# Attention with a threshold, then a feed-forward block: one eviction for both banks of a pair's turned queries or keys

## The chip, the cores and the metric

The kernel runs on one core of one Trainium2 chip. A core has a matrix engine (TensorE, PE in the profile; its weight loads stand apart as PEld), a vector engine (VectorE, DVE), a scalar engine (ScalarE, ACT), GpSimd (POOL) and a queue that issues most transfers (SyncE, SP). Each engine works through its own instructions in order, and waits on semaphores for the others. Matmul results land in PSUM, which has eight banks of 512 fp32 columns on 128 partitions; other engines evict them from there into on-chip memory (SBUF). The metric is the device time of one execution in microseconds (us).

## The reference

Everything is fp32. The attention keeps only scores within `tau` of their row's maximum:

```python
# q, k, v: batch 8, heads 8, sequence 576, head size 64
scores = scale * np.matmul(q, k.transpose(0, 1, 3, 2))       # scale = 1/8
thresh = np.max(scores, axis=-1, keepdims=True) - tau
scores = np.where(scores >= thresh, scores, -1000000000.0)
attn = np.exp(scores - np.max(scores, axis=-1, keepdims=True))
attn = attn / (np.sum(attn, axis=-1, keepdims=True) + 1e-09)
out = np.matmul(attn, v)
# the heads are joined to x: 4608 rows x 512
h = np.maximum(x @ w_in, 0.0)                                # w_in 512 x 2048
result = h * h @ w_out                                       # w_out 2048 x 512
```

## The kernel before

The first half of the time is the attention, the second the feed-forward block, which the change doesn't touch. All of this is about the attention.

Two heads of one batch make a *pair* (32 pairs). A *unit* is 128 query rows of a pair; a pair has four whole units, and the 64 queries that are left over from two neighbouring pairs share a fifth, so two pairs make nine units, 144 in all. In the code `FULL` is 4, `MAIN` 512, `REST` 64 and `HALF` 64. Units go two by two, an even one (A) and an odd one (B), through a pipeline of 72 *periods* and a few at its ends. What one period does for a unit is cut into named steps, and a step table says in which order the steps are written in the program; every engine meets its own part of them in that order. A `-` behind a step means that it belongs to the period before, `--` to the one before that. There are two tables. `CONVERTING` serves the first half of the attention (periods 2 to 34), in which weights are converted from wide floats on the side; `PLAIN` serves the rest. This is `PLAIN`, with steps among them that no later section speaks of:

```python
PLAIN = """
    put give fetch ahead eU-- powA0-- V-- powA1-- eV-- maskA1-- PV-- powB1-- c1- RA- powB0-- T--
    maskA0-- U- W-- Q-- x-- c4- maskB1-- SA- eT-- RB- maskB0-- topA0- over- topA1- c2 s2 leastA- eW--
    SB- topB0- s1- c5 c6 topB1- inv- leastB- xm-- c3
""".split()
```

The steps, with the lines that the profile shows them under:

- **T, the turn** (L423, TensorE). Scores need queries and keys with the head's 64 numbers on the partitions, so a pair's queries (8 transposes) or keys (10, with the left-over queries among them) are transposed into the middle columns of PSUM banks 1 and 4. One turn is done in most periods; 64 in all.
- **eT** (L428, L436, ACT) evicts the turn. Queries: two scaled copies of 256 columns (L428), one from each bank, which multiply by 1/8 and the sign. Keys: a copy of 256 columns from bank 1, one of 320 from bank 4 (L436), and a scaled copy of the 64 left-over queries from bank 1 (L428).
- **SA, SB** (L459, TensorE): a unit's scores against the first 512 keys. A's two heads land in banks 0 and 5, B's in banks 2 and 3. **RA, RB** (L459): against the last 64 keys, into the edges of banks 1 and 4, beside the main columns.
- **topA0 to topB1** (L477, DVE): copy a head's scores out of PSUM and give the row minimum of the negated scores. **pow** (L487, ACT) and **mask** (L492, DVE): exponential and threshold.
- **U, V** (L403, TensorE) transpose most of the weights into the two banks of a tile `pt`; **eU, eV** (L552, ACT) evict them. **W** (L403) transposes the rest into banks 2 and 3, **Q** (L542) spreads the row sums beside them, and **eW** (L552, from `sc`) evicts both.
- **PV** (L561, TensorE): weights times values, in banks 0 and 5. **x** (L708 ACT, L710 DVE) evicts the result, **xm** (POOL) scales it.

The tile `sc` is banks 0 to 5. Its order is kept by the function `touch`. Every instruction on `sc` reports there which banks it uses, as a range `on`. `touch` walks back through the last 300 reports of the other engines. An instruction whose banks don't overlap is declared independent; of those that overlap, the latest of each engine becomes a dependence, reads against reads too. The test for overlap is:

```python
if on[-1] < others[0] or others[-1] < on[0]:
```

It compares the first and the last bank of the two ranges.

## Time and profile before

| what | value |
|---|---|
| median of 3 runs | 1271.97 us (1270.42 to 1272.17) |
| span of the profiled execution, first to last instruction | 1273.4 us |
| attention, by the last values matmul | ends near 494 us |
| converting table | about 25 to 248 us |
| plain table | about 250 to 490 us |
| granted TensorE clock, mean | 0.996 |

The profiled execution's own time outside the span is not given on the page; its span is 1.4 us over the median of the plain runs. The profile has several views. The page gives each engine's busy time. The chain of waits follows the work that ended last back from the end, at each step to what released it. The timeline lists instructions in order of time, with neighbours of one kind merged; a bracket behind a row names how long the engine was idle before it and what ended that. Groups by shape gives count, busy time and mean length of one kind of instruction. Busy by stretch sums each engine over a window. A transpose or a score matmul in fp32 shows as two instructions, so counts on TensorE are twice those of the program. On ACT and DVE one row's start commonly lies about 0.1 us before the end of the row ahead, since the engine takes up the next while the last one's results still land.

### The profile page before, as it was taken

To read this page: it belongs to the slowest core of one execution; us is meant where nothing else is said; L and a number is where in the kernel's file an instruction comes from. 1 tells how busy PE (TensorE), PEld (TensorE's weight loads), DVE (VectorE), ACT (ScalarE), POOL (GpSimd) and SP (SyncE) were. 2 spreads that over 40 slices of the span, in tenths; PEclk is the share of its full clock that TensorE was granted. 3 is DMA by queue.
4 is the path that set the end of the run, shared out by engine and by line. 5 is a ranking of instruction groups with operands and counts; after the bars stand their busy time and mean duration, and the time that the engine had idled before them with its cause. 6 is when DMAs were issued, how large, how long until landed. Compare 5 with 4: busy or idle time off the path is not lost.

```text
span 1273.4 us, 55161 instructions
## 1 busy us (share of the span) xinstructions
PE 1251.7 (98%) x22991; PEld 1093.6 (86%) x22991; DVE 988.2 (78%) x2385; ACT 844.3 (66%) x1536; POOL 982.5 (77%) x1070
## 2 busy tenths in 40 slices
PE   8999999999999999999999999999999999999998
PEld 5777776777777778988888888999999999999998
DVE  6999998999999996886887878867746654665463
ACT  6999998999999994666765856675524432443240
POOL 2999998877776542988898989868787878787776
PEclk8999999999999999999999999999999999999999
DMA  7566677434333323657667657579965336533511
GB/s 186 143 161 154 167 198 188 120 89 107 89 81 89 83 53 97 192 166 237 202 191 231 215 169 249 172 274 369 267 163 152 83 107 163 146 84 107 167 35 35
DMA packets 289912, 196.79 MB, mean 155 GB/s; under 512 B 98560, under 2 KB 250624, under 8 KB 289664
## 3 DMA queue, kind: packets, MB, share of 16 engines
q1 hardware_dynamic: 288352, 192.86, 52.8%
q8 instruction: 181, 2.97, 1.0%
q14 instruction: 67, 0.55, 0.1%
q10 hardware_dynamic: 1312, 0.41, 0.1%
HBM read 120.85 MB, written 72.35 MB: 152 GB/s over the span
## 4 chain that ended last, share of the span: by engine, by line
PE 72%; DMA 3%; ACT 2%; POOL 2%; DVE 1%; issue 1%; DVEq 0%; ACTq 0%; POOLq 0%; SPq 0%
PE po L818 27%; PE ph L997 17%; PE ph L818 10%; PE sc L561 7%; PE sc L459 6%; PE pt L403 4%; PE sc L542 1%; PE sc L423 1%; POOL arena L126 1%; DMA g<-arena 1%; ACT arena L970 1%; DVE arena L126 1%; DMA w<-arena 1%; ACT arena L971 1%; ACT c L857 1%
## 5 line engine op out<-in xcount | busy, mean ns | idle before, releaser
L126 POOL TENSOR_TENSOR arena<-arena 128x512 f32<-128x512 f32 (+1 forms) x314 | 378.7, 1224 | 125.1 <-DVE arena L126 113.5
L818 PE MATMUL po<-wall,arena 128*64 128x128 f32 x7056 | 385.8, 273 | 1.4 <-ACT arena L813 0.8
L818 PEld LDWEIGHTS po<-wall,arena 128*64 128x64 f32 x7056 | 385.1, 137 | 1.9 <-ACT arena L813 1.0
L126 DVE TENSOR_TENSOR arena<-ph,arena 128x512 f32<-128x512 f32 x378 | 254.5, 688 | 77.4 <-PE ph L997 30.9
L123 POOL TENSOR_TENSOR arena<-arena 128x128 f32<-128x128 f32 (+1 forms) x322 | 265.5, 826 | 24.1 <-DMA arena<-w 8.5
L997 PE MATMUL ph<-arena,wall 128*128 128x256 f32 x1176 | 256.7, 380 | 2.3 <-DVE arena L126 2.1
L997 PEld LDWEIGHTS ph<-arena,wall 128*128 128x128 f32 x1176 | 222.4, 190 | 36.3 <-DVE arena L126 6.2
L126 DVE TENSOR_TENSOR arena<-po,arena 128x128 f32<-128x128 f32 x378 | 107.6, 288 | 159.3 <-PE po L818 151.4
L492 DVE SCALAR_TENSOR_TENSOR arena<-arena 128x576 f32<-128x576 f32 x288 | 225.9, 820 | 0.4 <-ACT arena L487 0.3
L487 ACT ACTIVATE arena<-arena 128x576 f32<-128x576 f32 x288 | 214.1, 781 | 13.4 <-DVE arena L477 13.3
L477 DVE TENSOR_SCALAR_CACHE_REDUCE arena<-sc 128x576 f32<-128x576 f32 x288 | 203.4, 752 | 18.5 <-ACT arena L552 5.7
L857 ACT COPY c<-arena 128x512 f32<-128x512 f32 (+1 forms) x295 | 168.9, 578 | 70.1 <-DVE arena L123 36.1
L459 PE MATMUL sc<-arena 64*64 64x512 f32 (+1 forms) x2304 | 179.6, 415 | 5.6 <-ACT arena L552 1.2
L561 PE MATMUL sc<-arena 64*64 64x128 f32 (+1 forms) x5760 | 165.6, 261 | 1.0 <-ACT arena L552 0.5
L123 DVE TENSOR_TENSOR arena<-arena,c 128x512 f32<-128x512 f32 x235 | 154.2, 664 | 12.1 <-ACT c L857 7.1
L561 PEld LDWEIGHTS sc<-arena 64*64 64x64 f32 x5760 | 150.4, 133 | 4.5 <-ACT arena L552 0.7
L552 ACT COPY arena<-pt 128x1024 f32<-128x1024 f32 x143 | 145.0, 1014 | 4.6 <-PE pt L403 3.9
L459 PEld LDWEIGHTS sc<-arena 64*64 64x64 f32 x2304 | 76.8, 134 | 71.4 <-issue 47.2
L813 ACT COPY arena<-po 128x128 f32<-128x128 f32 x63 | 16.6, 264 | 177.6 <-PE po L818 174.8
L818 PE MATMUL ph<-arena,wall 128*64 128x128 f32 x2352 | 129.2, 273 | 0.6 <-DVE arena L710 0.6
L818 PEld LDWEIGHTS ph<-arena,wall 128*64 128x64 f32 x2352 | 128.3, 137 | 1.4 <-issue 1.0
L484 POOL TENSOR_SCALAR arena<-arena,tau_p 128x2 f32<-128x2 f32 x144 | 83.8, 582 | 58.5 <-DVE arena L477 44.7
(55 smaller groups left out, 1142.5 us busy)
## 6 DMA issues: line engine op xcount, KB each, us to landing
gp<-arena SPq DMA_DIRECT2D x96, 256.0 KB, 3.4
arena<-gp SPq DMA_DIRECT2D x96, 256.0 KB, 5.4
w<-arena SPq DMA_DIRECT2D x60, 256.0 KB, 2.7
wall<-w SPq DMA_DIRECT2D x49, 256.0 KB, 5.3
g<-arena SPq DMA_DIRECT2D x48, 256.0 KB, 3.7
arena<-g SPq DMA_DIRECT2D x48, 256.0 KB, 5.0
arena<-w SPq DMA_DIRECT2D x44, 256.0 KB, 3.4
arena<-in_v_dram SPq DMA_DIRECT2D x32, 288.0 KB, 3.8
```

The costliest lines, as they stand in the source:

```text
L123: e.tensor_tensor(out=out, in0=x, in1=y, op=ALU.subtract)
L126: e.tensor_tensor(out=out, in0=x, in1=y, op=ALU.add)
L459: made = nc.tensor.matmul(sc[at, ds(to, count)], lhs, kT[rows, ds(at_k, count)], start=True, stop=True)
L477: made = nc.vector.tensor_scalar(out=s[:, j, :], in0=sc[:, ds(at, S)], scalar1=1.0, scalar2=None, op0=ALU.mult, op1=ALU.min, accum_out=nmx ...
L484: nc.gpsimd.tensor_scalar(out=thr, in0=nmx, scalar1=tau_p[:, :], scalar2=None, op0=ALU.add)
L487: nc.scalar.activation(out=w[:, :, j, :], in_=of(j), func=AF.Exp, bias=nmx[:, j : j + 1], scale=-1.0)
L492: nc.vector.scalar_tensor_tensor(out=w[:, :, j, :], in0=of(j), scalar=thr[:, j : j + 1], in1=w[:, :, j, :], op0=ALU.is_le, op1=ALU.mult, a ...
L552: touch(kind, copy_by(joined(to), whole(pt, 0, count)), at, 2 * BANK, m)
L561: made = nc.tensor.matmul(sc[ds(u * D, D), ds(5 * j * BANK + row, count)], loaded_v[i][rows, (c - (u != j)) % CH, :], wT[m][rows, ds(weigh ...
L818: nc.tensor.matmul(to[cols], lhs[:, cols], rhs, start=start, stop=stop, skip_group_check=True)
L857: nc.scalar.copy(c, y)
L997: nc.tensor.matmul(to[:, 2 * j : 2 * j + 2, :], W_IN[m, k][:, ts(2 * h + j, P)], part_x(steps, k, m), start=(not more and j == 0), stop=Tr ...
```

## The change

The two banks' pieces of a turn are evicted by one instruction. For this, keys and left-over queries share one tile: `kT` now has two parts of 320 columns, the first with 256 keys and the 64 left-over queries, the second with 256 keys and the last 64. The left-over queries are therefore copied unscaled, and the units that use them take their scale in the row minimum, from the tile `qscale` in place of the constant 1.0. Score matmuls read the first 512 keys as two pieces of 256 that lie 320 apart. The new eviction tells `touch` its banks with the pair `(1, 4)`. Only the very first keys' turn is still evicted in two pieces, one of them on DVE.

```diff
-                sb.tile([P, S], FP32, tag="kT", bufs=K_RING, name="kT"),
-                sb.tile([P, REST], FP32, tag="qR", bufs=K_RING, name="qR"),
+                sb.tile([P, MAIN + 2 * REST], FP32, tag="kT", bufs=K_RING, name="kT"),
...
-    def touch(what, made, at, size, key=0):
+    def touch(what, made, at, size, key=0, on=None):
...
-        on = range(at // BANK, (at + size - 1) // BANK + 1)
+        on = on or range(at // BANK, (at + size - 1) // BANK + 1)
...
-    def turn(i, which, spots, other=None):
+    def turn(i, which, spots, joint=None, other=None):
...
-        def scaled(to, spot):
-            touch(kind, nc.scalar.activation(out=to, in_=spot[0], func=AF.Identity, scale=qscale[:, :]), spot[1], BANK, i)
+        n = half + which * REST
+        into = to[which].rearrange("p (r n) -> p r n", r=2)
+        by_scale = lambda out, in_: nc.scalar.activation(out=out, in_=in_, func=AF.Identity, scale=qscale[:, :])
+        copies = [nc.scalar.copy if which else by_scale, other]
 
         def then():
-            part = lambda r, x, n: (spots[r][0][:, ds(x, n)], spots[r][1])
-            if which:
-                for r, n in ((0, half), (1, half + REST)):
-                    spot = part(r, 0, n)
-                    copy_by = other if r and other else nc.scalar.copy
-                    touch(kind, copy_by(to[1][:, ds(r * half, n)], spot[0]), spot[1], BANK, i)
-                scaled(to[2], part(0, half, REST))
-                ask_ahead(i, 1)
+            if joint is None:
+                for r, (spot, at) in enumerate(spots):
+                    touch(kind, copies[r](into[:, r, :], spot[:, 0:n]), at, BANK, i)
             else:
-                for r in range(2):
-                    scaled(to[0][:, ds(r * half, half)], part(r, 0, half))
-                ask_ahead(i, 0)
+                touch(kind, copies[0](into, joint[:, :, 0:n]), spots[0][1], BANK, i, (1, 4))
+            ask_ahead(i, which)
...
-                qT, kT, qR = turned[of[c]]
-                lhs = qT[rows, ds((c * FULL + t) * HALF, HALF)] if t < FULL else qR[rows, :]
+                qT, kT = turned[of[c]]
+                lhs = qT[rows, ds((c * FULL + t) * HALF, HALF)] if t < FULL else kT[rows, ds(MAIN // 2, REST)]
+                keys, into = kT[rows, ds(MAIN + REST, REST)], sc[at, ds(to, count)]
+                if not rest:
+                    keys = kT[rows, :].rearrange("p (r n) -> p r n", r=2)[:, :, 0 : MAIN // 2]
+                    into = into.rearrange("p (r n) -> p r n", r=2)
...
+        unscaled = qscale[:, :] if units[n][1] == FULL else 1.0
...
-                out=s[:, j, :], in0=sc[:, ds(at, S)], scalar1=1.0, scalar2=None,
+                out=s[:, j, :], in0=sc[:, ds(at, S)], scalar1=unscaled, scalar2=None,
...
-            free = None
+            free, both_ = None, sc.rearrange("p (r n) -> p r n", r=2)[:, :, ds(BANK + REST, (FULL + 1) * HALF)]
...
-            late["turn"] = [turn(g // 2, g % 2, free or spots()) for g in turns]
+            late["turn"] = [turn(g // 2, g % 2, free or spots(), both_) for g in turns]
```

No step changes its place in a table. What changes on the engines is which instruction waits for which. In the changed kernel line numbers are lower by one or two: L706 is the copy x, L550 the evictions eU, eV and eW, L485 the exponential, L458 the scores, L540 Q, L402 the weights' transposes; L436 and L428 are the new single evictions of keys and queries.

ACT before, in the plain table, from x of a period with a keys' turn to the exponentials of the next unit (the names in brackets are the engines whose semaphores an instruction waits for):

```order
L708 COPY arena<-sc 128x128 [waits DMAHW5_49,DMAHW4_49,PE_49]
L436 COPY arena<-sc 128x256 [waits PE_49]
L436 COPY arena<-sc 128x320 [waits PE_49]
L428 ACTIVATE arena<-sc,qscale 128x64
L552 COPY arena<-sc 128x2x4x64 [waits PE_49,Pool_49]
L552 COPY arena<-pt 128x2x8x64 [waits Activation_49]
L487 ACTIVATE arena<-arena 128x9x64 [waits DVE_49] x2
```

ACT now, at the same place:

```order
L706 COPY arena<-sc 128x128 [waits DMAHW5_49,DMAHW4_49,PE_49]
L436 COPY arena<-sc 128x640 [waits PE_49]
L550 COPY arena<-sc 128x2x4x64 [waits Pool_49]
L550 COPY arena<-pt 128x2x8x64 [waits Activation_49]
L485 ACTIVATE arena<-arena 128x9x64 [waits DVE_49] x2
```

Three evictions have become one. The two old ones waited for the last transposes of the turn into their bank; the wait of the new one is for the last matmul of Q, and eW behind it (L550 from `sc`) no longer waits for TensorE. Of the program's 72 such eW, 31 have lost that wait.

TensorE before, at the same place, from W to the first transposes of V:

```order
L403 MATMUL sc<-ident,arena 128x64 x4
L542 MATMUL sc<-ident,arena 64x64 [waits DVE_49]
L542 MATMUL sc<-ident,arena 64x64 x7
L459 MATMUL sc<-arena 64x512 [waits Activation_49]
L459 MATMUL sc<-arena 64x512
L459 MATMUL sc<-arena 64x512 [waits DVE_49]
L459 MATMUL sc<-arena 64x512
L459 MATMUL sc<-arena 64x64 [waits Activation_49]
L459 MATMUL sc<-arena 64x64
L459 MATMUL sc<-arena 64x64 [waits Activation_49]
L459 MATMUL sc<-arena 64x64
L459 MATMUL sc<-arena 64x512 [waits Activation_49]
```

TensorE now:

```order
L402 MATMUL sc<-ident,arena 128x64 x4
L540 MATMUL sc<-ident,arena 64x64 [waits DVE_49]
L540 MATMUL sc<-ident,arena 64x64 x7
L458 MATMUL sc<-arena 64x512 [waits Activation_49]
L458 MATMUL sc<-arena 64x512
L458 MATMUL sc<-arena 64x512 [waits DVE_49]
L458 MATMUL sc<-arena 64x512
L458 MATMUL sc<-arena 64x64 [waits Activation_49]
L458 MATMUL sc<-arena 64x64 x3
L458 MATMUL sc<-arena 64x512 [waits Activation_49]
```

Nothing moved: SA (two heads), RB, SB. RB waited for the evictions of banks 1 and 4 one by one and now waits once, for the one eviction; SB waits for eW, as before.

ACT before, in the converting table, at a queries' turn:

```order
L487 ACTIVATE arena<-arena 128x9x64 [waits DVE_49]
L487 ACTIVATE arena<-arena 128x9x64
L428 ACTIVATE arena<-sc,qscale 128x256 [waits DVE_49] x2
L708 COPY arena<-sc 128x128 [waits DMAHW4_49,DMAHW3_49,PE_49]
L708 COPY arena<-sc 128x128 [waits PE_49]
```

ACT now, at the same place:

```order
L485 ACTIVATE arena<-arena 128x9x64 [waits DVE_49]
L485 ACTIVATE arena<-arena 128x9x64
L428 ACTIVATE arena<-sc,qscale 128x512 [waits DVE_49]
L706 COPY arena<-sc 128x128 [waits DMAHW4_49,DMAHW3_49,PE_49]
L706 COPY arena<-sc 128x128 [waits PE_49]
```

Here each of the two old evictions waited for the row minimum that read its own bank, the third and the fourth of a period; the new one waits for the fourth.

More of the change, by code (lines that the diff above doesn't have):

```diff
@@ L450, in scores @@
         of, t = units[n]
-        at_k, count = (MAIN, REST) if rest else (0, MAIN)
+        count = REST if rest else MAIN
         for j in range(2):
@@ L456, in scores @@
                 rows, at = ds(j * D, D), ds(c * HALF, HALF)
-                qT, kT, qR = turned[of[c]]
-                lhs = qT[rows, ds((c * FULL + t) * HALF, HALF)] if t < FULL else qR[rows, :]
-                made = nc.tensor.matmul(
-                    sc[at, ds(to, count)], lhs, kT[rows, ds(at_k, count)], start=True, stop=True
-                )
+                qT, kT = turned[of[c]]
[4 more added lines that the diff above has]
+                    into = into.rearrange("p (r n) -> p r n", r=2)
+                made = nc.tensor.matmul(into, lhs, keys, start=True, stop=True)
                 touch("scores" if t < FULL else "last scores", made, to, count, of[c])
@@ L690, in turn_some @@
         def turn_some():
[L691 removed]
+            free, both_ = None, sc.rearrange("p (r n) -> p r n", r=2)[:, :, ds(BANK + REST, (FULL + 1) * HALF)]
             if turns and p < 2:
                 pq = pt_pool.tile([P, 2, BANK], FP32, tag="pt", name="pq")
[L694 to L695 removed]
+                free, both_ = [(pq[:, r, :], None) for r in range(2)], pq
+            late["turn"] = [turn(g // 2, g % 2, free or spots(), both_) for g in turns]
         def PV():
@@ L1203 @@
             pq = pt_pool.tile([P, 2, BANK], FP32, tag="pt", name="pq")
-            turn(0, 0, [(pq[:, r, :], None) for r in range(2)])()
+            turn(0, 0, [(pq[:, r, :], None) for r in range(2)], pq)()
             keep_busy(8, sc[:, ds(5 * BANK, P)])
-            turn(0, 1, spots(), nc.vector.tensor_copy)()
+            turn(0, 1, spots(), None, nc.vector.tensor_copy)()
             for p in range(FIRST_PERIOD, NU // 2 + 6):
```

1 line of the change is left out of this document (removed).

## The prediction

> **What bounds the kernel now.** I first read the busy shares by stretch, to part the attention half into its two step tables, then the chain of waits, then the timeline of single periods, and last the groups by shape for the durations. The two rows are the stretch of the converting table and of the plain table (columns: stretch and its length, then PE, PEld, DVE, ACT and POOL busy, granted clock, DMA share, GB/s).
>
> ```profile
> 60.00:180.00 120.00, 116.50 (x3031) 87.52 (x3024) 118.62 (x333) 117.65 (x217) 110.66 (x123) 1.00 0.65 165
> 255.00:466.00 211.00, 210.59 (x5691) 158.21 (x5695) 202.43 (x595) 198.85 (x340) 141.44 (x189) 1.00 0.38 87
> ```
>
> In the converting stretch DVE (118.62 of 120) and ACT (117.65) are both nearly full. In the plain stretch TensorE has 210.59 of 211, ACT 198.85. A busy TensorE alone proves little, since its ends are modelled, so I look at the chain over part of two plain periods (start, length, what):
>
> ```profile
> 321.00 0.46 PE sc L423 x10
> 321.45 0.50 PE pt L403 x16
> 321.95 0.12 PE sc L403 x4
> 322.08 0.39 PE sc L542 x16
> 322.47 1.85 PE sc L459 x24
> 324.32 0.64 PE pt L403 x16
> 324.96 2.24 PE sc L561 x68
> ```
>
> Each piece starts where the one before ends: turn (L423), U (L403), W (L403 into sc), Q (L542), scores SA, RB and SB (L459), V, values. No other engine is in the chain, so in the plain stretch anything that stops TensorE is added to the time, and anything that only relieves ACT is worth nothing there. ACT around the same keys' turn, then the TensorE rows that go with it, then DVE's first row minimum (timelines: start, length, engine, line, shapes):
>
> ```profile
> 321.59 0.25 ACT L708 COPY arena<-sc 128x128 f32<-128x128 f32 x1
> 321.74 0.71 ACT L436 COPY arena<-sc 128x256 f32<-128x256 f32 x2
> 322.32 0.34 ACT L428 ACTIVATE arena<-sc,qscale 128x64 f32<-128x64 f32 x1
> 322.59 0.58 ACT L552 COPY arena<-sc 128x512 f32<-128x512 f32 x1
> 323.07 1.02 ACT L552 COPY arena<-pt 128x1024 f32<-128x1024 f32 x1
> 324.35 0.78 ACT L487 ACTIVATE arena<-arena 128x576 f32<-128x576 f32 x1 [0.27 <-DVE arena L477]
> ...
> 322.01 0.46 PE L542 MATMUL sc<-ident,arena 64*64 64x64 f32 x16
> 323.26 0.63 PE L459 MATMUL sc<-arena 64*64 64x512 f32 x4
> 324.25 0.28 PE L403 MATMUL pt<-ident,arena 64*128 64x64 f32 x2
> ...
> 323.55 0.76 DVE L477 TENSOR_SCALAR_CACHE_REDUCE arena<-sc 128x576 f32<-128x576 f32 x1 [0.24 <-issue]
> ```
>
> The reader is to see that today the turn's three evictions fill exactly the time in which TensorE does U, W and Q: they begin at 321.74, long before Q ends at 322.47, and are over at 322.66. Then eW (L552 from sc) starts at 322.59, 0.12 after Q's end; SB starts at 323.26, after eW's end at 323.17; and V at 324.25, after eU's end at 324.09. DVE waits 0.24 and ACT 0.27 a period; they have that much to spare.
>
> **The change, part by part.** *The new wait, plain stretch.* The order rows in the section on the change show the cause. The one eviction is noted as lying on banks 1 to 4, which takes in banks 2 and 3, where W and Q write just ahead of it in program order. Its wait for TensorE is therefore for Q's last matmul and not for the turn's; eW, which carries that wait today (where nothing stands ahead of it, it idles for Q, 2.6 us in all in the groups below), has lost it. Behind the waiting eviction on ACT stand eW and eU, and SB waits for eW, V for eU. The durations, from the groups of ACT over 255 to 466 us and one group of the whole run:
>
> ```profile
> L552 ACT COPY arena<-pt 128x1024 f32<-128x1024 f32 x66 | 66.3, 1005 | 0.0
> L552 ACT COPY arena<-sc 128x512 f32<-128x512 f32 x33 | 19.3, 585 | 3.0 <-PE sc L542 2.6
> L428 ACT ACTIVATE arena<-sc,qscale 128x256 f32<-128x256 f32 x30 | 12.7, 477 | 0.0
> L436 ACT COPY arena<-sc 128x320 f32<-128x320 f32 x15 | 6.6, 440 | 0.0
> ...
> L813 ACT COPY arena<-ph 128x512 f32<-128x512 f32 x63 | 36.7, 582 | 81.4 <-PE ph L997 37.3 <-PE ph L818 35.1 <-DVE arena L126 8.9
> ```
>
> Copies of 512 and 1024 columns take 0.585 and 1.005 us, so a column costs 0.82 ns. The keys' eviction of 640 columns is then 0.585 + 128 x 0.82 ns = 0.69 us, the scaled queries' of 512 is 0.477 + 256 x 0.82 ns = 0.69 us as well. A copy of 512 columns out of two banks (L552, 585 ns) costs what one out of a single bank does (L813, 582), so I add nothing for the second bank. What a restart of TensorE costs is shown where ACT is late today, at the first plain turn (ACT, then two rows of TensorE):
>
> ```profile
> 252.60 0.61 ACT L552 COPY arena<-sc 128x512 f32<-128x512 f32 x1
> ...
> 253.26 0.66 PE L459 MATMUL sc<-arena 64*64 64x512 f32 x4
> 254.28 0.34 PE L403 MATMUL pt<-ident,arena 64*128 64x64 f32 x4
> ```
>
> SB restarts 0.05 after eW's end (253.21), and V follows 1.02 after SB's start, against 0.99 when nothing stopped (323.26 to 324.25). So for the period at 322: the eviction starts where eW did, 322.59; ends 323.28; eW starts 0.10 before that end, as eU does after eW, at 323.18; ends 323.76; SB 323.81; V 324.83 in place of 324.25. That is 0.58 us a period. RB also waits for the eviction (323.33 in place of 323.15), inside the same stall. eU ends at 323.76 - 0.10 + 1.02 = 324.68 and still clears V. A queries' turn has the same sum, since its eviction lasts as long. Nothing gives the 0.58 back, since TensorE had no idle to fill. Turns in this stretch: the 30 scaled 256-wide pieces are 15 queries' turns, the 15 copies of 320 are 15 keys' turns: 30 x 0.58 = 17.4 us. The turn at 252, where ACT was late anyway (eW 0.34 after Q's end, not 0.12), pays about 0.4. Together +17.8 us.
>
> *Converting stretch.* Here the eviction's order holds it behind DVE's fourth row minimum, which read banks 3 and 4. Of a keys' turn and of the queries' turn after it, today (ACT, DVE, TensorE), and the count of the pieces between 30 and 248 us:
>
> ```profile
> 123.51 0.68 ACT L436 COPY arena<-sc 128x256 f32<-128x256 f32 x2
> 124.08 0.33 ACT L428 ACTIVATE arena<-sc,qscale 128x64 f32<-128x64 f32 x1
> 122.91 0.75 DVE L477 TENSOR_SCALAR_CACHE_REDUCE arena<-sc 128x576 f32<-128x576 f32 x1
> 124.46 0.46 PE L423 MATMUL sc<-ident,arena 64*128 64x64 f32 x8
> ...
> 130.28 0.84 ACT L428 ACTIVATE arena<-sc,qscale 128x256 f32<-128x256 f32 x2
> 129.69 0.75 DVE L477 TENSOR_SCALAR_CACHE_REDUCE arena<-sc 128x576 f32<-128x576 f32 x1
> 131.16 0.54 PE L423 MATMUL sc<-ident,arena 64*128 64x64 f32 x10
> ...
> L428 ACT ACTIVATE arena<-sc,qscale 128x256 f32<-128x256 f32 x28 | 11.7, 469 | 0.2 <-DVE arena L477 0.2
> L436 ACT COPY arena<-sc 128x320 f32<-128x320 f32 x14 | 6.1, 437 | 0.0
> ```
>
> The first piece now starts at 123.51, before that row minimum ends at 123.66; only the second must wait for it. The one eviction starts 0.04 after it (L487 starts 0.04 after the minimum that ends at 324.31), at 123.70, and ends at 124.39, where three pieces ended at 124.41. For queries: 130.44 + 0.04 + 0.69 = 131.17 against 131.12. The next turn on TensorE starts 0.05 behind the eviction: 124.44 against 124.46, and 131.22 against 131.16. So -0.02 and +0.06, with 14 keys' turns and 28 / 2 = 14 queries': 14 x 0.04, +0.5 us. ACT's shorter work is eaten by the later start.
>
> *The scale in the row minimum.* 32 row minima take their factor from a tile. The nearest row is the mask, which has such a factor and a second input:
>
> ```profile
> L492 DVE SCALAR_TENSOR_TENSOR arena<-arena 128x576 f32<-128x576 f32 x126 | 97.7, 812 | 0.0
> L477 DVE TENSOR_SCALAR_CACHE_REDUCE arena<-sc 128x576 f32<-128x576 f32 x126 | 90.1, 751 | 6.2 <-ACT arena L487 3.5 <-ACT arena L552 1.8 <-issue 0.4
> ```
>
> Between 0 and 0.06 us each; some 14 of them lie in the converting stretch, where DVE has no cover (0 to 0.9 us); in the plain one its 0.24 us of waiting covers them. I take 0, since the second input is the likelier cause of the 0.06.
>
> *Keys in two pieces.* SB's pass of 512 columns takes 0.45 us from start to start at 323.26 (next pass 323.71). L997 already streams two pieces that lie apart, 256.7 us for 1176 matmuls of 256 columns, 0.22 each: the same rate. Cost 0.
>
> ```profile
> 323.71 0.61 PE L459 MATMUL sc<-arena 64*64 64x512 f32 x4
> L997 PE MATMUL ph<-arena,wall 128*128 128x256 f32 x1176 | 256.7, 380 | 2.3 <-DVE arena L126 2.1
> ```
>
> *Start-up and the second half.* Four turns come before these stretches, with other tiles and unbusy engines: 0 to -0.5, taken as 0. The feed-forward half has the same instructions, later.
>
> Sum: 17.8 + 0.5 = +18.3 us. The profiled execution spans 1273.4 us, 1.4 above the median of the plain runs (1271.97), so 1291.7 for its span and 1290.3 for the median.
>
> **A rule against this.** The Trainium skill, page "PSUM — Partial Sum Buffer", section on bank collisions, says that PSUM is to be guarded by bank and quadrant, and that accesses to different banks run clean. By it an eviction of banks 1 and 4 need not wait for work in 2 and 3, and the plain stretch would pay nothing; no run here shows which accesses are safe. It describes what a wait must cover; the order rows show what this program waits for, and those decide. It is the page behind the first rival.
>
> **Rivals.** (1) *Held by its own two banks alone.* The eviction would start 0.15 after x as today, plain turns would cost 0, and in the converting stretch ACT would be relieved and the next turn would come earlier; DVE's 6.2 us of idle there is the most that could be won, about 2 of it likely (the rest are a few long single waits): 1270. It decides if the eviction begins before Q ends. For it: the two banks are named. Against: 31 eW rows without a TensorE wait, as many as plain turns. 4%. (2) *Part is absorbed.* If the plain chain had hidden slack as large as ACT's own wait (0.27), a turn would cost 0.31: 30 x 0.31 + 0.5, 1282. Against it the chain is without a gap. 6%. (3) *The merged eviction saves nothing*: it lasts as long as the pieces' rows together, 0.92 (321.74 to 322.66) and 0.84 (the row at 130.28), 0.88 in the mean: +0.19 over 30 and 28 turns, 11 more, 1301. Half of that, 1296, is as far as I go. 5%. (4) *The granted clock falls* because TensorE now idles: 1.00 to, say, 0.96 over the plain stretch's 230 us would be 9 us, 1299. Against: 1.00 in the converting stretch, with TensorE idle for 3.5 of 120 us. 3%. My forecast: 82%.
>
> **How the numbers follow.** The likeliest is 1290.3. If a merged eviction took only the 0.585 of the 512-wide copy, 0.105 less over 58 turns would be 6 less, 1284.3. Upward I go half way to rival 3. The range 1284.5 to 1296 leaves out rivals 1, 2 and 4 and the far half of 3, some 15%. 0.2% is 2.5 us, about what a measurement here can tell from no change. Slower than that is all but rival 1: 95%; rival 1 gives faster 3% and same 2%.
>
> **What would show it.** Between 255 and 466 us of the old times: the merged eviction with about 0.6 us of idle before it, released by Q; its mean 690 ns; SB waiting about 0.55 for eW in each turn's period; TensorE busy near 92%; a turn's period 6.9 us and one without a turn unchanged; the converting stretch within 1 us. It is wrong if the eviction starts before Q ends, or if the plain stretch is not 15 us or more longer.

## The result and the profile after

| | before | after |
|---|---|---|
| median, us | 1271.2 (1269.9 to 1272.17) | 1283.73 (1281.84 to 1284.54) |
| span of the profiled execution, us | 1273.4 | 1280.1 |
| ratio, 95% interval | | 1.0100 (1.0086 to 1.0113) |

The changed kernel is 12.5 us slower, where 18.3 was forecast (1290.3 over a median of 1271.97 at the time, range 1284.5 to 1296.0). The span of after is 1.7 us shorter than its execution (1281.84 us, the shortest of its four); with the same 1.7 the profiled execution of before took, by estimate, about 1275 us, longer than any of its four. So the two spans differ by 6.7 us only; the comparison goes by the medians, and below by lengths inside single periods.

Busy by stretch after, the two stretches of the prediction, with the same columns:

```profile
60.00:180.00 120.00, 116.52 (x2990) 86.76 (x2986) 118.17 (x331) 116.13 (x191) 110.08 (x124) 1.00 0.64 166
255.00:466.00 211.00, 206.69 (x5406) 144.95 (x5402) 192.76 (x566) 182.49 (x281) 136.47 (x180) 1.00 0.37 86
```

In the plain stretch fewer instructions run in the same 211 us on every engine (TensorE 5406, before 5691), and DVE and ACT are busy for 192.76 and 182.49 us, before 202.43 and 198.85. TensorE's busy time fell by 4 us only. The granted clock is 1.00 as before. In the converting stretch little moved. The chain of waits over one period with a keys' turn shows what is new in the plain stretch:

```profile
321.86 0.46 PE sc L422 x8
322.32 0.50 PE pt L402 x15
322.82 0.12 PE sc L402 x4
322.94 0.43 PE sc L540 x16
323.38 0.02 issue
323.40 0.69 ACT arena L436
324.09 0.50 ACT arena L550
324.59 0.04 issue
324.63 1.09 PE sc L458 x8
325.72 0.64 PE pt L402 x16
326.37 2.14 PE sc L559 x68
```

T, U, W and Q follow each other as before, but between Q and SB (the last eight L458) the chain now runs over ACT: the one eviction (L436), then eW (L550). Before, no other engine stood in it. The timeline of ACT at this place, between TensorE's rows of Q and of V, with the columns of the prediction:

```profile
322.87 0.46 PE L540 MATMUL sc<-ident,arena 64*64 64x64 f32 x16
...
323.40 0.69 ACT L436 COPY arena<-sc 128x640 f32<-128x640 f32 x1 [0.88 <-PE sc L540]
...
323.99 0.59 ACT L550 COPY arena<-sc 128x512 f32<-128x512 f32 x1
...
324.46 1.03 ACT L550 COPY arena<-pt 128x1024 f32<-128x1024 f32 x1
...
325.65 0.71 PE L402 MATMUL pt<-ident,arena 64*128 64x64 f32 x16
```

And the groups by shape of ACT over 255 to 466 us:

```profile
L550 ACT COPY arena<-sc 128x512 f32<-128x512 f32 x32 | 18.7, 584 | 1.9 <-PE sc L540 1.9
L428 ACT ACTIVATE arena<-sc,qscale 128x512 f32<-128x512 f32 x15 | 10.3, 687 | 14.0 <-PE sc L540 14.0
L436 ACT COPY arena<-sc 128x640 f32<-128x640 f32 x14 | 9.7, 692 | 11.8 <-PE sc L540 11.8
```

The 29 evictions wait for Q (L540), 0.84 us in the mean for keys and 0.93 for queries, and last 0.69 us. From the first values matmul of one period to that of the next, the median over the plain stretch is 6.74 us, before 6.36. The stall is where it was forecast, but a period with a turn is 0.37 to 0.38 us longer, not 0.58. Two kinds of period differ. One period in nine has no turn: it is 0.16 us shorter than before (6.07, before 6.23). The first period with a turn behind it is 0.53 longer (6.81, before 6.28, at 420 us of after; the two others in the stretch hold single long waits). The last periods, which have no turn and none in front of them, keep their 6.03 and 6.05. So a stall costs some 0.53 us, and the period behind it gives 0.16 back.

Where it is given back, behind the stall, is seen in the values, with which a period begins here. Busy by stretch for the values' matmuls alone (stretch of 0.05 us and its length, TensorE busy with the matmuls in flight in brackets, weight loads, clock, DMA), before, where PV begins:

```profile
324.88:324.93 0.05, 0.04 (x1) 0.04 (x1) 1.00 0.61 103
324.93:324.98 0.05, 0.05 (x1) 0.05 (x2) 1.00 0.23 52
324.98:325.03 0.05, 0.05 (x1) 0.05 (x2) 1.00 0.04 10
325.03:325.08 0.05, 0.05 (x5) 0.05 (x4) 1.00 0.00 0
```

And after:

```profile
326.28:326.33 0.05, 0.04 (x4) 0.04 (x4) 1.00 0.17 41
326.33:326.38 0.05, 0.05 (x4) 0.05 (x8) 1.00 0.29 67
326.38:326.43 0.05, 0.05 (x6) 0.05 (x10) 1.00 0.23 51
```

Before, a single matmul is under way for 0.15 us, and only then the other quarters of the array join in. After, four start at once. What the others waited for stands in DVE's timeline, the first and the second row minimum of unit A, before:

```profile
323.55 0.76 DVE L477 TENSOR_SCALAR_CACHE_REDUCE arena<-sc 128x576 f32<-128x576 f32 x1 [0.24 <-issue]
...
324.24 0.75 DVE L477 TENSOR_SCALAR_CACHE_REDUCE arena<-sc 128x576 f32<-128x576 f32 x1
```

and after:

```profile
324.60 0.76 DVE L475 TENSOR_SCALAR_CACHE_REDUCE arena<-sc 128x576 f32<-128x576 f32 x1 [0.60 <-ACT arena L550]
...
325.29 0.75 DVE L475 TENSOR_SCALAR_CACHE_REDUCE arena<-sc 128x576 f32<-128x576 f32 x1
```

The second row minimum reads bank 5, and half of the values' matmuls write to bank 5. Before, it ended at 324.24 + 0.75 = 324.99, 0.10 after PV began at 324.89; after, at 326.04, 0.25 before PV begins at 326.29. The bracket on the first row minimum of after names eW, but eW stands behind it in the program; in both traces this minimum starts 0.11 after the end of RB's last matmul (323.44 and 324.49). So in the kernel before two branches ran side by side from RB to the values: TensorE's own (SB, V) and DVE's (two row minima), and DVE's was the longer by some 0.16 us (from the start of bank 0's matmuls to that of bank 5's in the trace's records, in 27 of the 33 periods from 255 to 466 us; at the end of a period without a turn the first values matmul itself comes 0.19 later). A stall ahead of the values uses this time up, and the values then run 0.16 shorter (2.35 to 2.20 us from their first start to their last end, medians). TensorE showed no gap for it, since one quarter of the array was busy meanwhile. That became the theory which the runs tested.

### The profile page after: what moved, and what is told of

Read it like the earlier page. It is cut to its first block, busy times and chain, and to the rows that moved or that the text cites. A ratio compares the mean times of both kernels' runs of the same rounds, so it can differ in the third digit from the quotient of the medians.

```text
span 1280.1 us, 55008 instructions
## 1 busy us (share of the span) xinstructions
PE 1255.8 (98%) x22991; PEld 1086.7 (85%) x22991; DVE 989.5 (77%) x2385; ACT 834.7 (65%) x1441; POOL 982.0 (77%) x1070
## 4 chain that ended last, share of the span: by engine, by line
PE 73%; ACT 7%; DVE 6%; POOL 5%; issue 4%; DMA 4%; SPq 1%; POOLq 0%; ACTq 0%; DVEq 0%
PE po L816 27%; PE ph L995 16%; PE ph L816 10%; PE sc L559 7%; PE sc L458 5%; PE pt L402 4%; DVE arena L475 3%; DVE arena L490 2%; ACT arena L550 2%; PE sc L540 1%; PE sc L422 1%; POOL arena L126 1%; ACT arena L428 1%; DMA w<-arena 1%; POOL wall L216 1%
## 5 line engine op out<-in xcount | busy, mean ns | idle before, releaser
L485 ACT ACTIVATE arena<-arena 128x576 f32<-128x576 f32 x288 | 213.2, 777 | 5.4 <-DVE arena L475 5.4
L475 DVE TENSOR_SCALAR_CACHE_REDUCE arena<-sc 128x576 f32<-128x576 f32 x256 | 181.1, 753 | 24.2 <-ACT arena L550 18.0
L458 PE MATMUL sc<-arena 64*64 64x512 f32 (+1 forms) x2304 | 185.9, 417 | 10.3 <-ACT arena L550 2.4
L123 DVE TENSOR_TENSOR arena<-arena,c 128x512 f32<-128x512 f32 x235 | 154.3, 665 | 10.7 <-ACT c L855 6.9
L559 PE MATMUL sc<-arena 64*64 64x128 f32 (+1 forms) x5760 | 160.4, 261 | 0.5 <-ACT arena L550 0.5
L559 PEld LDWEIGHTS sc<-arena 64*64 64x64 f32 x5760 | 145.7, 133 | 3.5 <-ACT arena L550 0.7
L550 ACT COPY arena<-pt 128x1024 f32<-128x1024 f32 x143 | 144.9, 1013 | 2.5 <-PE pt L402 1.8
L458 PEld LDWEIGHTS sc<-arena 64*64 64x64 f32 x2304 | 71.7, 133 | 87.5 <-issue 36.7
```

What stands on the lines that cost most here:

```text
L123: e.tensor_tensor(out=out, in0=x, in1=y, op=ALU.subtract)
L458: made = nc.tensor.matmul(into, lhs, keys, start=True, stop=True)
L475: made = nc.vector.tensor_scalar(out=s[:, j, :], in0=sc[:, ds(at, S)], scalar1=unscaled, scalar2=None, op0=ALU.mult, op1=ALU.min, accum_ou ...
L485: nc.scalar.activation(out=w[:, :, j, :], in_=of(j), func=AF.Exp, bias=nmx[:, j : j + 1], scale=-1.0)
L550: touch(kind, copy_by(joined(to), whole(pt, 0, count)), at, 2 * BANK, m)
L559: made = nc.tensor.matmul(sc[ds(u * D, D), ds(5 * j * BANK + row, count)], loaded_v[i][rows, (c - (u != j)) % CH, :], wT[m][rows, ds(weigh ...
```

## The experiments

Each run stands beside runs of the kernel before on the same chip; the ratios are to those. "Plain period" is the median over the plain stretch from the first values matmul to the next period's, by the trace.

**1. The layout without the one eviction.** Everything of the change but its last step: turns are evicted by two instructions.

```diff
-            if joint is None:
+            if joint is None or spots[0][1] is not None:
                 for r, (spot, at) in enumerate(spots):
-                    touch(kind, copies[r](into[:, r, :], spot[:, 0:n]), at, BANK, i)
+                    touch(kind, (copies[r] or copies[0])(into[:, r, :], spot[:, 0:n]), at, BANK, i)
```

> The changed kernel's layout (keys and left-over queries in one tile of two parts, left-over queries unscaled, the scale in the row minimum, the first 512 keys read as two pieces), but every turn is evicted by two instructions, each ordered by its own bank alone. Theory (the time is lost because the one eviction waits for Q, and nothing else of the change costs): the plain stretch is as before, and a keys' turn is evicted by two copies of 320 columns in place of three pieces, so 1270 to 1272 us, against 1271.2 before; the first eviction of a plain turn starts about 0.15 us after x, without a wait for Q. Rival (the layout costs: strided keys, the pointer scale or the shared tile): near the changed kernel's 1283.7, at least 1276.

Measured 1270.03 us, ratio 0.9989 (0.9973 to 1.0006), plain period 6.36. The shared tile, the strided keys and the scale taken from a tile cost nothing that the time shows. The scale does cost its instruction something; DVE's groups by shape over the whole run:

```profile
L475 DVE TENSOR_SCALAR_CACHE_REDUCE arena<-sc 128x576 f32<-128x576 f32 x256 | 180.7, 751 | 12.5 <-ACT arena L550 4.8 <-issue 3.8 <-PE sc L458 3.2
L475 DVE TENSOR_SCALAR_CACHE_REDUCE arena<-sc,qscale 128x576 f32<-128x576 f32 x32 | 24.8, 812 | 1.9 <-ACT arena L550 1.1 <-issue 0.7
```

A row minimum with its factor from a tile takes 0.06 us more. Where both minima of a unit A have it, once in nine plain periods, the next period is 6.48 us long in place of 6.36; the plain stretch has four such periods, 0.5 us in all.

**2. The wait without the one eviction.** The kernel before, with its pieces told that they lie on banks 1 to 4.

```diff
-    def touch(what, made, at, size, key=0):
+    def touch(what, made, at, size, key=0, on=None):
...
-        on = range(at // BANK, (at + size - 1) // BANK + 1)
+        on = on or range(at // BANK, (at + size - 1) // BANK + 1)
...
-            touch(kind, nc.scalar.activation(out=to, in_=spot[0], func=AF.Identity, scale=qscale[:, :]), spot[1], BANK, i)
+            touch(kind, nc.scalar.activation(out=to, in_=spot[0], func=AF.Identity, scale=qscale[:, :]), spot[1], BANK, i, (1, 4))
...
-                    touch(kind, copy_by(to[1][:, ds(r * half, n)], spot[0]), spot[1], BANK, i)
+                    touch(kind, copy_by(to[1][:, ds(r * half, n)], spot[0]), spot[1], BANK, i, (1, 4))
```

> The kernel before with all its separate evictions of turns, of which each but the first two is noted as lying on banks 1 to 4, so that it waits for Q like the changed kernel's one eviction. Theory (the wait is what costs): slower than the changed kernel, since three pieces of 0.92 us (keys) or two of 0.84 (queries) now stand between Q and eW in place of one of 0.69: some 0.2 us more in each of 30 plain turns, 6 us over 1283.7, and up to 4 in the converting stretch, so 1287 to 1294. Rival (it is the merging, two banks in one instruction, that costs): 1271 to 1273.

Measured 1291.46 us, ratio 1.0153 (1.0129 to 1.0177), plain period 6.95. ACT's groups by shape over 255 to 466 us in this run:

```profile
L428 ACT ACTIVATE arena<-sc,qscale 128x256 f32<-128x256 f32 x28 | 11.7, 470 | 12.3 <-PE sc L542 12.3
...
L436 ACT COPY arena<-sc 128x256 f32<-128x256 f32 x14 | 5.2, 372 | 12.2 <-PE sc L542 12.2
```

The wait for Q is there (12.2 us in 14 turns) without any merging, and the time is worse than with it by 7.7 us: the wait alone costs, and the merging takes part of it back. Per plain period the difference to the changed kernel is 6.95 - 6.74 = 0.21 us, as the lengths say (0.92 or 0.84 against 0.69).

**3. Work put into the hidden wait.** V repeats its first transposes in every plain period but the first; two slots are four transposes.

```diff
+    AGAIN, plain = 2, [False]
+
...
-        for i, (u, c) in enumerate(FIRST[first : first + count]):
+        again = AGAIN if f == "V" and plain[0] else 0
+        for i, (u, c) in list(enumerate(FIRST[first : first + count]))[0:again] + list(enumerate(FIRST[first : first + count])):
...
+        plain[0] = not BEGIN_WITH.get(p) and not converts(p)
```

> The kernel before, in which V repeats its first two transposes of each head in every plain period but the first ones (four more transposes, about 0.12 us of TensorE work; the result is the same). Theory (in the kernel before, the values' matmuls on bank 5 wait for DVE's second row minimum, about 0.16 us in each of 37 plain periods, hidden in a TensorE that shows no gap): the repeats lie in that wait, so +0 to +1 us, 1271 to 1272.5. Rival (TensorE's plain chain has no slack, as the prediction had it): 37 x 0.12 = +4.5 us, 1275.7.

Measured 1271.06 us, ratio 0.9999 (0.9984 to 1.0013), plain period 6.35. From V's start to PV's start the trace has 0.767 us where it had 0.642, and from there to the end of the values 0.125 less. The values' matmuls at PV's start in this run, in the same view as above:

```profile
321.54:321.59 0.05, 0.04 (x1) 0.04 (x1) 1.00 0.10 21
321.59:321.64 0.05, 0.05 (x4) 0.05 (x5) 1.00 0.00 0
```

The lone matmul's time has shrunk from 0.15 us to less than 0.05. TensorE was given 0.125 us more work in 37 periods, 4.6 us in all, and the time stood still. With ten transposes (`AGAIN = 5`):

> The kernel before, in which V repeats ten transposes in every plain period but the first (about 0.31 us of TensorE work; the result is the same). With four repeats (0.125 us) the time stood still. Theory (TensorE's branch from RB over SB and V to the values has 0.16 us to spare against DVE's branch over the two row minima, and no more): 37 x (0.31 - 0.16) = +5.5 us, 1276.6, between 1275 and 1278; the values' matmuls on bank 5 start with those on bank 0, no longer 0.16 us behind. Rival (the slack is larger, or of another kind): below 1274; no slack at all: 37 x 0.31 = +11.5, 1282.5.

Measured 1274.33 us, ratio 1.0029 (1.0015 to 1.0044): 1.9 to 5.6 us more. That is just below the expected 1275 to 1278, with the forecast 5.5 at the interval's edge. In the trace the plain period is 6.51, longer by the forecast 0.15; 37 x 0.15 is 5.5, so some 2 us of it did not reach the median, and where they stayed is open. No slack at all (+11.5) is out, and so is a slack that covers 0.31 us.

**4. The same work in the changed kernel**, the same edit:

> The changed kernel with the same four repeated transposes of V in 37 plain periods. Theory (the wait of the values for the row minimum has been used up by the stall ahead of it in the 30 periods with a turn): 30 x 0.12 and little in the 7 others, +3.7 to +4.6 us, so 1287.4 to 1288.3 against the changed kernel's 1283.7. Rival (the hidden wait was never there, and the plain periods lost less for another reason): the same step here as in the kernel before, whatever its size.

Measured 1286.43 us, ratio 1.0109 (1.0089 to 1.0129). That is 2.7 us over the changed kernel's 1283.73, less than forecast, and the two intervals overlap, so the time alone decides nothing. In the trace the plain period went from 6.74 to 6.86, by the whole 0.12: the wait that hid the repeats in the kernel before is used up.

**5. The one eviction in the plain table alone.**

```diff
-                    touch(kind, copies[r](into[:, r, :], spot[:, 0:n]), at, BANK, i)
+                    touch(kind, (copies[r] or copies[0])(into[:, r, :], spot[:, 0:n]), at, BANK, i)
...
+            both_ = None if p > 1 and converts(p) else both_
             late["turn"] = [turn(g // 2, g % 2, free or spots(), both_) for g in turns]
```

> The changed kernel, in which the turns of the converting table are evicted by two instructions, each ordered by its own bank, and only the plain table keeps the one eviction. Theory (the plain stretch carries nearly all of the loss: 30 periods that are 0.37 us longer): 11 us over the kernel before, 1281 to 1283, with the converting stretch as before or a little shorter. Rival (the converting stretch has a fair part of the loss): below 1279.

Measured 1282.99 us, ratio 1.0088 (1.0071 to 1.0104): 11.5 us over the median of the kernel before beside it (1271.5), and plain period 6.74. The plain stretch carries the loss. What is left for the converting stretch, 12.5 - 11.5 = 1.0 us, is within the intervals.

**6. The turn behind W and Q.** That the one eviction be ordered by banks 1 and 4 alone was not tried, so no run shows what that would give. The order was changed instead, so that the last work on banks 1 to 4 ahead of the eviction is the turn itself, with U and SA to hide in:

```diff
-        put give fetch ahead eU-- powA0-- V-- powA1-- eV-- maskA1-- PV-- powB1-- c1- RA- powB0-- T--
-        maskA0-- U- W-- Q-- x-- c4- maskB1-- SA- eT-- RB- maskB0-- topA0- over- topA1- c2 s2 leastA- eW--
+        put give fetch ahead eU-- powA0-- V-- powA1-- eV-- maskA1-- PV-- powB1-- c1- RA- powB0-- W-- Q-- T--
+        maskA0-- U- x-- c4- maskB1-- SA- eW-- eT-- RB- maskB0-- topA0- over- topA1- c2 s2 leastA-
```

> The changed kernel with its plain table written in another order: W and Q go before T in TensorE's program, and eW goes before the turn's one eviction in ACT's. The eviction then waits for T alone, which is now the last to write banks 1 to 4 ahead of it, and has U and SA (about 1.36 us) to hide in before RB needs its banks. Theory (the loss is the wait for Q with the eviction's length behind it): the plain periods are back at their old length, and only the converting stretch keeps its +1 or so: 1270 to 1274. Rival (the one eviction of two banks costs something by itself in the plain stretch): 1277 to 1284.

Measured 1280.99 us, ratio 1.0075 (1.0061 to 1.0088), plain period 6.66: the rival's number. The chain of waits in this run tells why it is not the rival's reason:

```profile
322.78 0.27 PE sc L402 x4
323.05 0.39 PE sc L540 x16
323.44 0.46 PE sc L422 x10
323.90 0.50 PE pt L402 x16
324.39 2.00 PE sc L458 x24
```

ACT is gone from the chain. But W's four transposes take 0.27 us where they took 0.12 behind U, and the scores 2.00 where they took 1.85 behind Q: 0.30 us, the whole difference of the period (6.66 against 6.36). In both places the tile's shape now changes, from 64*64 (RA) to 64*128 (W) and from 64*128 (U) to 64*64 (SA). The Trainium skill, page "TensorEngine Tiling (Array Packing)", section "Key Properties", says that a change of tiling mode drains the engine. The rows agree in so far as TensorE loses time at both places; they put it at about 0.15 us each. So the order was written once more with Q, which has RA's shape, ahead of W (Q, now the first of the two, names their banks):

```diff
-        put give fetch ahead eU-- powA0-- V-- powA1-- eV-- maskA1-- PV-- powB1-- c1- RA- powB0-- T--
-        maskA0-- U- W-- Q-- x-- c4- maskB1-- SA- eT-- RB- maskB0-- topA0- over- topA1- c2 s2 leastA- eW--
+        put give fetch ahead eU-- powA0-- V-- powA1-- eV-- maskA1-- PV-- powB1-- c1- RA- powB0-- Q-- W-- T--
+        maskA0-- U- x-- c4- maskB1-- SA- eW-- eT-- RB- maskB0-- topA0- over- topA1- c2 s2 leastA-
...
         def Q():
             if has(2 * m + 2):
+                pt["W"] = two_banks(w_bank(m + 1))
```

> As the kernel with the turn after W and Q, but Q stands ahead of W: in TensorE's plain order RA, Q, W, T, U, SA. The earlier order (RA, W, Q, T, U, SA) left no wait for ACT, but changed between tiles of 64 and of 128 columns four times a period ahead of SA, in place of two, and each change shows 0.15 us from start to start where 0.06 or less is usual. Theory (that run's loss was these changes, 2 x 0.09 us in 37 plain periods, and not the one eviction): some 6 to 7 us less than its 1281.0, 1272 to 1275. Rival (the one eviction costs in the plain stretch wherever it stands): 1279 to 1282.

Measured 1275.71 us, ratio 1.0042 (1.0026 to 1.0058), plain period 6.48. The order before it lost 9.5 us to the kernel before, this one 4.7 (1270.99 beside it): half is gone with two changes of shape, less than forecast. From the first values matmul to SA a period with a keys' turn takes 3.72 us, with the order before it 4.02. The rest shows in ACT's timeline:

```profile
326.01 0.59 ACT L550 COPY arena<-sc 128x512 f32<-128x512 f32 x1
326.50 0.70 ACT L436 COPY arena<-sc 128x640 f32<-128x640 f32 x1
```

eW goes first, and the eviction ends at 327.20; RB starts at 327.25 in the trace's records, 0.98 us after SA where it is 0.86 in the kernel before. The 0.12 us equal the whole difference of the period. So RB still waits for the eviction, only less.

**7. RB with RA.** If DVE's branch closes the periods of the kernel before, RB done earlier could shorten it.

```diff
-        put give fetch ahead eU-- powA0-- V-- powA1-- eV-- maskA1-- PV-- powB1-- c1- RA- powB0-- T--
-        maskA0-- U- W-- Q-- x-- c4- maskB1-- SA- eT-- RB- maskB0-- topA0- over- topA1- c2 s2 leastA- eW--
+        put give fetch ahead eU-- powA0-- V-- powA1-- eV-- maskA1-- PV-- powB1-- c1- RA- RB- powB0-- T--
+        maskA0-- U- W-- Q-- x-- c4- maskB1-- SA- eT-- maskB0-- topA0- over- topA1- c2 s2 leastA- eW--
```

> The kernel before, in which the plain table does RB right after RA, ahead of the turn, in place of between SA and SB. DVE's first row minimum then waits for SA, not for RB, and can start about 0.11 us earlier. Theory (in the kernel before, plain periods are closed by a loop over TensorE and DVE: RB, first and second row minimum, the values' matmuls on bank 5, with 0.16 us in it that TensorE could do without): 37 x 0.11 = 4 us faster, 1266 to 1268. Rival (TensorE's chain alone sets the plain periods): no change, 1271, since TensorE has the same work.

Measured 1272.48 us, ratio 1.0004 (0.999 to 1.0018), plain period 6.36: a miss. The chain of waits in this run:

```profile
320.58 2.13 PE sc L561 x67
...
322.88 0.24 PE sc L459 x13
323.12 0.39 PE sc L423 x8
```

The values take 2.13 us, 0.11 less than the 2.24 of the chain before, so the wait did shrink as forecast. But the rest-key scores behind them have grown by RB. The loop that closes the period runs from the values on bank 5 over RA, T, U, W, Q and SA to the two row minima and back to bank 5; RB left one place in it and came into another. The row minimum fits this: it starts 0.11 us after the end of RB's last matmul in the kernel before, and here 0.11 after that of SA's. The forecast took the branch for the loop.

The same with two evictions a turn, and RB ahead of T in the converting table as well:

```diff
-        put give fetch ahead eU-- powA0-- V-- powA1-- eV-- maskA1-- PV-- powB1-- c1- RA- powB0-- T--
-        maskA0-- U- W-- Q-- x-- c4- maskB1-- SA- eT-- RB- maskB0-- topA0- over- topA1- c2 s2 leastA- eW--
+        put give fetch ahead eU-- powA0-- V-- powA1-- eV-- maskA1-- PV-- powB1-- c1- RA- RB- powB0-- T--
+        maskA0-- U- W-- Q-- x-- c4- maskB1-- SA- eT-- maskB0-- topA0- over- topA1- c2 s2 leastA- eW--
...
-        x- T powB0- SA RB W- maskA1- c3 c4 inv- Q- c6- topA0 eV- topA1 leastA U xm- maskB0- powB1- eW- eU
+        x- RB T powB0- SA W- maskA1- c3 c4 inv- Q- c6- topA0 eV- topA1 leastA U xm- maskB0- powB1- eW- eU
```

> The kernel with two evictions a turn, each ordered by its own bank, with RB right after RA in the plain table and ahead of the turn in the converting table. Theory: in the plain stretch as with RB early there (4 us); in the converting stretch, too, the first row minimum starts 0.33 us after RB's last matmul in every period, so up to 33 x 0.11 = 3.6 us more: 1262 to 1266, faster than both kernels. Rival (TensorE's chain alone): 1270.

Measured 1277.61 us, ratio 1.0045 (1.0032 to 1.0059), 7.6 us over experiment 1, and again a miss. Its converting periods have a median of 6.94 us, there 6.81; plain ones 6.36 as there. TensorE's timeline in the converting stretch of experiment 1, from V to W, with the tile's shape behind the operation:

```profile
122.68 0.71 PE L402 MATMUL pt<-ident,arena 64*128 64x64 f32 x16
123.23 0.41 PE L422 MATMUL sc<-ident,arena 64*128 64x64 f32 x8
123.58 1.20 PE L458 MATMUL sc<-arena 64*64 64x512 f32 x16
124.71 0.34 PE L402 MATMUL sc<-ident,arena 64*128 64x64 f32 x4
```

and here:

```profile
117.00 0.71 PE L402 MATMUL pt<-ident,arena 64*128 64x64 f32 x16
117.64 0.34 PE L458 MATMUL sc<-arena 64*64 64x64 f32 x8
117.92 0.52 PE L422 MATMUL sc<-ident,arena 64*128 64x64 f32 x10
118.37 1.09 PE L458 MATMUL sc<-arena 64*64 64x512 f32 x8
119.39 0.34 PE L402 MATMUL sc<-ident,arena 64*128 64x64 f32 x4
```

V to W takes 119.39 - 117.00 = 2.39 us for the same work that takes 2.03 there (of the 0.36, about 0.1 is this turn's two more transposes): RB between V and T adds two changes of shape, and two at the 0.15 of experiment 6 are about what is left.

**8. One eviction where hardly anything waits for it.** Q, W, T as in the second order of experiment 6, and RB beside RA, once with one eviction, once with two:

```diff
-        put give fetch ahead eU-- powA0-- V-- powA1-- eV-- maskA1-- PV-- powB1-- c1- RA- powB0-- T--
-        maskA0-- U- W-- Q-- x-- c4- maskB1-- SA- eT-- RB- maskB0-- topA0- over- topA1- c2 s2 leastA- eW--
+        put give fetch ahead eU-- powA0-- V-- powA1-- eV-- maskA1-- PV-- powB1-- c1- RA- RB- powB0-- Q-- W-- T--
+        maskA0-- U- x-- c4- maskB1-- SA- eW-- eT-- maskB0-- topA0- over- topA1- c2 s2 leastA-
...
         def Q():
             if has(2 * m + 2):
+                pt["W"] = two_banks(w_bank(m + 1))
```

> The kernel with TensorE's plain order RA, Q, W, T, U, SA, in which RB, too, goes right behind RA: RA, RB, Q, W, T, U, SA, SB, with one eviction for a turn. Theory: the first row minimum waits for SA, 0.11 us earlier, so that the values wait less for the second row minimum, and SB doesn't wait for eW, which comes some 0.8 us earlier: of the 0.16 us hidden in a plain period 0.1 to 0.15 comes free, 37 x 0.1 to 0.15 = 4 to 5.5 us under the kernel with RB in its old place: 1267 to 1271. Rival (TensorE's chain alone sets the period): equal to that kernel, 1272 to 1275.

> The same order (RA, RB, Q, W, T, U, SA, SB), with two evictions a turn, each ordered by its own bank. Theory: in the plain stretch as with the one eviction, since neither stands in TensorE's way there; in the converting stretch 1 to 2 us less, as between the changed kernel (13 us over the kernel before) and the one with the one eviction in the plain table alone (11.5): 1266 to 1270, and the fastest of all. Rival: equal to 1270.0, the kernel with two evictions and the old order.

Measured 1271.33 us, ratio 1.0002 (0.9989 to 1.0015), with one eviction, and 1271.57, ratio 1.0007 (0.9993 to 1.0022), with two. The one eviction costs nothing by itself that the time shows, and brings nothing either. Both times lie just above what was expected. Its groups by shape over 255 to 466 us, in the first of the two:

```profile
L436 ACT COPY arena<-sc 128x640 f32<-128x640 f32 x15 | 10.5, 698 | 0.0
L428 ACT ACTIVATE arena<-sc,qscale 128x512 f32<-128x512 f32 x15 | 10.4, 694 | 0.0
```

The same instructions as in the changed kernel, now without any wait of their own (in some periods SB still starts 0.05 us behind the eviction's end, 0.02 to 0.03 later than in the others). With RB in front, the loop of experiment 7 has the same work as before, and 6.37 us is the period again. The reason given in the forecast is not what happened: the values still wait 0.16 to 0.18 us for the second row minimum in most periods, so the hidden time did not come free; what is gone is the wait of RB for the eviction. None of these kernels is measurably faster than the kernel before; the nearest to it is experiment 1.

## Why the prediction was wrong in size

- **What bounds the plain stretch.** Half right. TensorE's chain has no gap in the view, and what stops TensorE does cost. But the chain names one predecessor at each step, and TensorE counts as busy while one quarter of its array works. Beside its branch (SB, V) lay DVE's, 0.16 us longer. Experiment 3 shows it: 0.125 us of added work cost nothing, and 0.31 lengthened the period by 0.15.
- **The cause of the wait** (held by Q, through the range 1 to 4). Right: all 29 evictions in the groups name Q, and experiment 2 has the wait alone and loses 20 us.
- **The eviction's length**, 0.69 us for both kinds. Right: 692 and 687 ns.
- **Its start**, "where eW did, 322.59". Wrong by 0.05 us: it starts 0.07 after Q's end (323.33, to 323.40), eW started 0.12 after it. Before, eW stood behind the scaled copy until 322.66, so its start was not that of Q's release.
- **eW 0.10 ahead of the eviction's end, SB 0.05 behind eW, V 1.02 behind SB.** Right: 323.99 against 324.09; 324.63 against 324.58; 325.65 - 324.63 = 1.02.
- **"Nothing gives the 0.58 back, since TensorE had no idle to fill."** This is the step that failed. V came 325.65 - 323.33 = 2.32 us after Q's end, before 324.25 - 322.47 = 1.78: 0.54 lost. Then the values, which no longer wait for the second row minimum, gave 0.16 back. The period lost 6.74 - 6.36 = 0.38, and over all kinds of periods with a turn 0.37. Of the missing 0.20, 0.04 is the start and 0.16 is what the values gave back. The term of 30 x 0.58 = 17.4 is 30 x 0.37 = 11.1; experiment 5 measured 11.5 for it and the turn at 252 together.
- **Converting stretch, +0.5.** 12.5 - 11.5 = 1.0 us is left for it, too near to the error to part the two.
- **Scale, pieces, start-up, 0.** Right for the time within -3.4 to +0.8 us, by experiment 1. The reason given for the scale was wrong: it put the mask's 0.06 us down to its second input, but a row minimum with its factor from a tile takes 812 ns, the mask's figure, without one. Nor did DVE's 0.24 us of waiting cover it in the plain stretch (6.48 us against 6.36).
- **The rivals.** The second (part is absorbed, 1282) was the nearest, with a slack of 0.27 assumed and 0.16 found; it was given 6%, with "the chain is without a gap" against it, which is the reading that fell. The first, third and fourth fell with the wait for Q, the 0.69 us and the clock of 1.00. The range ended 0.8 us above the time because absorption was left outside of it.
- **The signs.** By one of them the prediction was wrong: the plain stretch was to be 15 us or more longer, and from the first values matmul at 254.9 to that at 471.6 (252.4 to 479.8 after) it is 10.7 longer. A turn's period of 6.9 us was 6.74, and one without a turn did not stay unchanged (6.23 to 6.07).
- **TensorE busy near 92%**, as a sign, failed: 206.69 of 211 is 98%. Matmul ends are modelled, and of the 0.54 us in this period only 0.14 shows as idle, from RB's recorded end at 324.49 to SB at 324.63; so a fall of busy time does not measure such a stall; the period does. The idle time before the eviction was 0.84 to 0.93 us, not 0.6.

## What to carry to other kernels

Before a stall on the bounding engine is multiplied by its count, look at what runs beside that engine between the place of the stall and the next point where both meet: a second branch that ends later there takes part of the stall, though the chain and the busy share show neither a gap nor a second engine. The order of instructions on TensorE has a price of its own, in changes of the tile's shape. And when an order is kept by ranges, two banks with others between them are held by what lies between, so one instruction in place of two can wait for more than the two did.

## What the hardware showed

- A change of the tile's shape between 64*64 and 64*128 cost TensorE about 0.15 us here: 0.27 against 0.12 for the same four transposes, 2.00 against 1.85 for the same scores (experiment 6).
- TensorE passes as busy while one quarter of its array works and the matmuls behind wait: 0.15 us in which one matmul ran alone show no gap, in 27 of 33 plain periods.
- A row minimum of 576 columns took 751 ns with a constant factor and 812 ns with one read from a tile (experiment 1).
- An eviction of 2 x 320 columns from two banks took 692 ns, as 0.82 ns a column forecast; the second bank cost nothing that shows.
